# A one-core attention and MLP kernel: the second matrix product of the last eight chunks by Strassen's scheme, in two passes of its own

## The chip, the cores and the metric

The kernel runs on one core of a Trainium2 chip. The time is the device time of one execution in microseconds (us), with the median of several runs. Five engines work side by side and wait for each other through semaphores: PE (matmuls; its weight loads are shown apart as PEld), DVE and ACT (element-wise work), POOL, and SP, which here only issues DMAs. Every engine carries out its instructions in order.

## The reference

```python
for b in range(nb):                       # linear attention with decay, 4 x 8 heads, 768 x 64
    intra = einsum('bhic,bhjc->bhij', qb, kb) * Dmask
    out[:, :, sl] = einsum('bhij,bhjd->bhid', intra, vb) + einsum('bhid,bhde->bhie', qb * lam_pow, kv_state)
    kv_state = lam_block * kv_state + einsum('bhsd,bhse->bhde', kb_dec, vb)
x = out as 3072 tokens x 512
h = x @ w_in                              # 512 x 2048
g = maximum(h, 0) ** 2
return g @ w_out                          # 2048 x 512
```

## The kernel before

The 3072 tokens are 24 chunks of 128 (`t`); four chunks that are worked on together have a number `m` (0 to 5). The 2048 hidden features are 16 blocks of 128 (`f`). For precision each fp32 operand of a matmul is held as a high part in the matmul format fp32r and a low part, and a product is three matmuls: high x high, high x low, low x high. The weights lie so in `wh` and `wl` in SBUF: slots 0 to 15 for w_in, the others for w_out (`w_out(f)`, L106).

For m = 0 and 1 (chunks 0 to 7) `hidden` (L389) makes h of one f with 12 matmuls and `project` (L417) adds g @ w_out of that f into four PSUM banks `acc` with another 12 of 512 columns. For chunks 8 to 15 (m = 2 and 3 together) and 16 to 23 (m = 4 and 5) the first product goes by Strassen's scheme: `quad` (L561) takes a pair of f and pairs of neighbouring chunks as a 2 x 2 block product and needs seven products (`product`, L547, six matmuls of 512 columns each) where eight would stand. The sums of w_in blocks come from DRAM (`ws`) through a ring of eight tiles (`ring`, `stream`, tag "raw" of the pool `wk`), a load per product, eight products ahead. A quad ends with h of the even chunks in two PSUM banks, pa and pb, which ACT turns into g (Relu, Square) and DVE into a high and a low part (`square`, `rest`), and with g of the odd chunks kept in SBUF (`gs`). p1 is a copy of the first product; DVE adds it to others (u2, u3, and into pb). Between the products stand the projections of the quad before; the odd chunks are projected afterwards, f by f (`again`, then `project`), and in that stretch of m = 3 the attention of the next eight chunks is done.

The order on each engine is the order in which the code calls the operations. A tile of a pool takes one of the places of its tag, and what first writes it waits until the place's tile before is done with; tag "A" of `wk` has two places. When an m is through, `project` copies the four banks into two tiles o of tag "A" (`stage`; ACT takes banks 0 and 2, DVE 1 and 3) and SP stores them. This last `project` of an m runs inside the next `quad`, between its second and third product. Its p1 has tag "a".

Of the kernel before, what the change touches and what calls it, by code (L numbers as in the profile page):

```python
# [7 lines left out]
F32 = mybir.dt.float32  # L8
# [7 lines left out]
P = 128  # L16
B, H, S, D = 4, 8, 768, 64
C = 128
# [17 lines left out]
def body(ctx: ExitStack, tc: tile.TileContext, qT, kT, kvq, lam, w, out):  # L36
# [526 lines left out]

    def quad(n, m, prev, then=None):
# [22 lines left out]
        add(gs[1], pd, u3)  # L587
        rest(m, f, pa, gh)
# [5 lines left out]
        gh = square(pb)  # L594
        add(gs[0], pd, u2)
        rest(m, f + 1, pb, gh)
        for x in gs[::-1]:
            V.scalar_tensor_tensor(out=x, in0=x, scalar=0.0, in1=x, op0=ALU.max, op1=ALU.mult)  # L598
        project(m, f)
        return m, f + 1  # L600

# [217 lines left out]
    for m in range(2, NM, 2):  # L819
        more = m + 2 < NM  # L820
        first_t, last_t = (m + 2) * G, (m + 4) * G - 1
        for n in range(NF // 2):
            then = (lambda: load_kv(first_t)) if more and n == NF // 2 - 1 else None
            prev = quad(n, m, prev, then)
        again(m + 1, 0)
        if more:
            load_kv(first_t + 1)
            prep_k(first_t)
            scores(first_t, ps_a, "att")
            prep_q(first_t)  # L830
            masked(first_t)
        for f in range(NF):
            t = first_t + f // 2
            i, odd_ = f // 4, f // 2 % 2
            project(*prev)
            prev = (m + 1, f)
            if more and f % 2 == 0:
                if not odd_:
                    pack = wk.tile([P, 2, DM], F32, name="pack", tag="raw")
                KEPT[t] = pack[:, odd_]  # L840
                if t < last_t:
                    attend(t, ps_h, "h", t + 1)
                else:
                    attend(t, ps_a, "att")
                if t + 2 <= last_t:
                    load_qk(t + 2)
                    load_kv(t + 2)
            if f + 1 < NF:
                again(m + 1, f + 1)
            if more:  # L850
                if f % 2 == 0:
                    ahead(f + 1, t, last_t)
                    behind(f + 1, t, last_t)
                if f % 4 == 1:
                    part(*even(i, t))
                if f % 4 == 2:
                    part(*near(i, t - 1))
# [3 lines left out]
        if more:  # L861
            open_ring()
# [54 lines left out]
```

## Time and profile before

| | |
|---|---|
| median of 3 runs | 606.29 us (606.08 to 606.29) |
| the profiled execution | 606.06 us |
| its span, first to last instruction | 604.4 us |
| granted PE clock | 1.00 |
| PE, PEld, DVE, ACT, POOL busy | 98%, 81%, 58%, 39%, 15% |

The page's first part gives each engine's busy time, the fourth the chain of work that ended last, the fifth groups of instructions (line, engine, operation, output<-inputs, shape, count, busy us, mean ns of one, idle time before them and what ended it). A row of a timeline has the start, the length, the instruction and its count. The stretch with chunks 16 to 23 (m = 4 and 5) begins at about 435 us. A matmul's length is its time in the pipeline; the next one starts before it has ended.

### The profile page before, as it was taken

Reading aid. Unit: us, or ns where it says so; the run is one execution under the profiler, and the core shown is the slowest. Engines: PE = TensorE matmul, PEld = TensorE weight load, DVE = VectorE, ACT = ScalarE, POOL = GpSimd, SP = SyncE. Lnnn points to the kernel's source line nnn. Section 1 sums busy time; section 2 is a strip of 40 time slices with the busy share of each in tenths; the row PEclk is TensorE's granted clock in tenths of the full one; section 3 lists DMA queues with packets and bytes.
Section 4 is the critical chain, followed back from the end, with each engine's and each line's share of the span. In section 5 each row is a group of like instructions: output and inputs, shape, how many; then the busy total and the mean of one; then the engine's idle time right before and its main releaser. Section 6 shows DMA issues by size and latency. Waiting matters only on the chain.

```text
span 604.4 us, 9423 instructions
## 1 busy us (share of the span) xinstructions
PE 595.0 (98%) x3694; PEld 491.0 (81%) x3694; DVE 351.0 (58%) x535; ACT 235.6 (39%) x383; POOL 88.2 (15%) x95
## 2 busy tenths in 40 slices
PE   8989999999999999999999999999999999999997
PEld 6877888888888888888888888888888888888885
DVE  6899999938575677644444445766554444445222
ACT  4667887724333345432222222323332222223222
POOL 5411222323221231000000002243100000000000
PEclk9999999999999999999999999999999999999999
DMA  8766667227678674544444404432284444421001
GB/s 297 296 209 210 191 228 233 88 89 266 230 248 286 226 239 156 175 125 123 126 125 125 143 9 167 140 121 90 71 279 124 123 123 124 126 77 70 1 1 69
DMA packets 50107, 92.88 MB, mean 154 GB/s; under 512 B 5008, under 2 KB 19344, under 8 KB 50064
## 3 DMA queue, kind: packets, MB, share of 16 engines
q1 hardware_dynamic: 50064, 92.29, 47.6%
q8 instruction: 29, 0.48, 0.3%
q14 instruction: 14, 0.11, 0.1%
HBM read 71.30 MB, written 20.97 MB: 153 GB/s over the span
## 4 chain that ended last, share of the span: by engine, by line
PE 92%; DVE 5%; POOL 1%; ACT 1%; issue 0%; POOLq 0%; DVEq 0%
PE h L555 18%; PE acc L425 14%; PE acc L430 14%; PE acc L426 14%; PE h L395 13%; PE att L555 7%; PE att L279 3%; PE h L318 2%; PE h L325 2%; DVE A L138 1%; PE h L310 1%; DVE wl L153 1%; DVE A L144 1%; PE att L318 1%; DVE A L131 1%; PE att L325 1%
## 5 line engine op out<-in xcount | busy, mean ns | idle before, releaser
L425 PE MATMUL acc<-wh,gh 128*128 128x512 f32 x384 | 151.0, 393 | 0.0
L426 PE MATMUL acc<-wl,gh 128*128 128x512 f32 x384 | 149.5, 389 | 0.0
L430 PE MATMUL acc<-wh,gl 128*128 128x512 f32 x384 | 149.3, 390 | 0.0
L402 ACT ACTIVATE h<-h 128x512 f32<-128x512 f32 x64 | 37.3, 582 | 182.8 <-PE h L555 76.3
L555 PE MATMUL h<-wh,ring 128*128 128x512 f32 x320 | 85.5, 389 | 0.0
L425 PEld LDWEIGHTS acc<-wh,gh 128*128 128x128 f32 x384 | 72.0, 188 | 16.4 <-issue 0.5
L430 PEld LDWEIGHTS acc<-wh,gl 128*128 128x128 f32 x384 | 72.1, 188 | 15.7 <-DVE gl L410 0.5
L426 PEld LDWEIGHTS acc<-wl,gh 128*128 128x128 f32 x384 | 72.1, 188 | 14.6
L410 DVE TENSOR_TENSOR gl<-h,gh 128x512 fp32r<-128x512 f32 x64 | 44.1, 690 | 66.9 <-ACT h L405 66.8
L555 PEld LDWEIGHTS h<-wh,ring 128*128 128x128 f32 x320 | 60.1, 188 | 12.5
L208 DVE TENSOR_TENSOR kv_sb<-h,a 128x512 f32<-128x512 f32 x32 | 22.1, 691 | 64.7 <-PE h L555 63.1
L555 PE MATMUL h<-wl,ring 128*128 128x512 f32 x160 | 49.2, 389 | 0.0
L410 DVE TENSOR_TENSOR gl<-gs,gh 128x512 fp32r<-128x512 f32 x32 | 23.5, 736 | 42.5 <-ACT gh L605 42.0
L292 POOL TENSOR_TENSOR kv_sb<-kv_sb,mask 128x512 f32<-128x512 f32 x18 | 22.2, 1234 | 122.1 <-DVE gs L598 108.8
L404 ACT ACTIVATE gh<-h 128x512 fp32r<-128x512 f32 x64 | 38.4, 600 | 2.0
L405 ACT ACTIVATE h<-h 128x512 f32<-128x512 f32 x64 | 38.0, 594 | 0.0
L605 ACT CAST gh<-gs 128x512 fp32r<-128x512 f32 x32 | 19.9, 622 | 45.0 <-PE acc L426 45.0
L286 POOL TENSOR_TENSOR qk_sb<-qk_sb,qpow 128x512 f32<-128x512 f32 x18 | 27.0, 1500 | 68.9 <-PE att L279 67.9
L395 PE MATMUL h<-xh,wh 128*128 128x512 f32 x128 | 36.0, 403 | 0.0
L555 PEld LDWEIGHTS h<-wl,ring 128*128 128x128 f32 x160 | 30.0, 188 | 6.2
L395 PE MATMUL h<-xh,wl 128*128 128x512 f32 x128 | 34.5, 391 | 0.4 <-DVE wl L153 0.4
L395 PE MATMUL h<-xl,wh 128*128 128x512 f32 x128 | 34.3, 390 | 0.0
(141 smaller groups left out, 775.0 us busy)
## 6 DMA issues: line engine op xcount, KB each, us to landing
ring<-ws SPq DMA_DIRECT2D x112, 256.0 KB, 2.8
raw<-in_w SPq DMA_DIRECT2D x32, 512.0 KB, 4.6
kv_sb<-in_kvq SPq DMA_DIRECT2D x22, 512.0 KB, 5.2
ws<-parts SPq DMA_DIRECT2D x32, 256.0 KB, 2.7
out_x<-o SPq DMA_DIRECT2D x24, 256.0 KB, 2.2
qk_sb<-in_kT SPq DMA_DIRECT2D x22, 256.0 KB, 3.5
qk_sb<-in_qT SPq DMA_DIRECT2D x22, 256.0 KB, 4.2
ws<-wh SPq DMA_DIRECT2D x8, 256.0 KB, 5.2
```

What stands on the lines that cost most here:

```text
L208: lambda o, x, y, op=op: V.tensor_tensor(out=o, in0=x, in1=y, op=op)
L286: nc.gpsimd.tensor_tensor(out=feat[t][:, 1], in0=feat[t][:, 1], in1=qpow, op=ALU.mult)
L292: nc.gpsimd.tensor_tensor(out=x, in0=x, in1=y.broadcast_to([P, NPR, 2, D]), op=ALU.mult)
L395: nc.tensor.matmul(h, wt[:, f, kt * P : (kt + 1) * P], x[:, kt], start=k == 0, stop=k == 11)
L402: nc.scalar.activation(h, h, AF.Relu)
L404: nc.scalar.activation(gh, h, AF.Square)
L405: nc.scalar.activation(h, h, AF.Square)
L410: V.tensor_tensor(out=gl, in0=r, in1=gh.bitcast(F32), op=ALU.subtract)
L425: nc.tensor.matmul(accs[m][i], gh[:, cs], wh[:, j], start=f == 0, stop=False)
L426: nc.tensor.matmul(accs[m][i], gh[:, cs], wl[:, j], start=False, stop=False)
L430: nc.tensor.matmul(accs[m][i], gl[:, cs], wh[:, j], start=False, stop=end)
L555: nc.tensor.matmul(bank, x[:, part_, kt], t[:, q + kt], start=start and z == 0, stop=stop and z == 5, skip_group_check=True,)
```

## The change

Three things change.

1. **Chunks 8 to 15**: every `quad` gets a `fold(n)`: DVE rebuilds the two w_out blocks of the pair of f and makes four sums of their column halves, ACT (`fold_hi`) and DVE (`fold_lo`) split them into high and low parts, and SP stores both to DRAM (`wt`).
2. **Chunks 16 to 23, first product**: `quad_all` takes the place of `quad`. It projects nothing but the last of m = 3; g of the even chunks goes into SBUF places that are free by then (`E`; two of them through a tile "kept" and a DMA). Its p1 has tag "A".
3. **Chunks 16 to 23, second product**: `gather_all`, after all eight pairs, replaces the `project` calls of m = 4 and 5. Two passes (even chunks, odd chunks), in each eight pairs of f, seven products per pair, each of them six matmuls of 256 columns into one of seven banks. `operands` makes four sums of blocks of g, `operands_hi` and `operands_lo` their high and low parts, two pairs ahead and in three places of the old w_in slots; the w_out sums come back from `wt` through the two "raw" places, two pairs ahead. At the end of a pass seven adds form the output from the banks.

```diff
+    wt = dram.tile([NF // 2, P, 4, 2, 2 * P], F32, name="wt")
+    FOLD = {}
+
+    def fold(n):
+        rec = wk.tile([P, 2, 2, 2 * P], F32, name="rec", tag="A")
+        for i in range(2):
+            j = w_out(2 * n + i)
+            add(rec[:, i].rearrange("p b c -> p (b c)"), f32(wh[:, j]), f32(wl[:, j]))
+        x = wk.tile([P, 4, 2 * P], F32, name="sums", tag="A")
+        (b11, b12), (b21, b22) = ([rec[:, i, j] for j in range(2)] for i in range(2))
+        T1, T2, T3, T4 = (x[:, i] for i in range(4))
+        sub(T1, b12, b11)
+        sub(T2, b22, T1)
+        sub(T3, b22, b12)
+        sub(T4, b21, T2)
+        FOLD[n] = x
+
+    def fold_hi(n):
+        nc.scalar.copy(wh[:, NF - 2 : NF].rearrange("p a d -> p (a d)"), FOLD[n].rearrange("p a b -> p (a b)"))
+
+    def fold_lo(n):
+        hi, lo = (t[:, NF - 2 : NF].rearrange("p a d -> p (a d)") for t in (wh, wl))
+        sub(lo, FOLD.pop(n).rearrange("p a b -> p (a b)"), f32(hi))
+        for i, x in enumerate((hi, lo)):
+            nc.sync.dma_start(out=wt[n, :, :, i], in_=f32(x).rearrange("p (a b) -> p a b", a=4))
+
     def quad(n, m, prev, then=None):
...
         add(gs[1], pd, u3)
+        fold(n)
...
+        fold_hi(n)
...
+        fold_lo(n)
         project(m, f)
...
+    def square_to(f, h):
+        x = wk.tile([P, N], F32, name="kept", tag="A") if f in (2, 3) else E[f]
+        nc.scalar.activation(h, h, AF.Relu)
+        nc.scalar.activation(x, h, AF.Square)
+        if f in (2, 3):
+            nc.sync.dma_start(out=E[f], in_=x)
+
+    def places_for(f):
+        if f == 0:
+            E.extend(wk.tile([P, N], F32, name="kept", tag="a") for _ in range(2))
+            E.extend(f32(t[:, NF - 1]) for t in (wh, wl))
+            E.extend(mask.rearrange("p j a c -> p j (a c)")[:, j] for j in range(2))
+            E.extend(x.rearrange("p a c -> p (a c)") for x in (qpow, kv))
+        if f in (8, 10):
+            x = io.tile([P, 2 * DM], F32, name="qk_sb")
+            E.extend(x[:, j * DM : (j + 1) * DM] for j in range(2))
+        if f >= 12:
+            for _ in range(2):
+                E.append(wk.tile([P, N], F32, name="kept", tag="gh" if f == 12 else "gl"))
+
+    def quad_all(n, prev):
+        f = 2 * n
+        last = n == NF // 2 - 1
+        if n % 2 == 0:
+            G_of[n // 2] = wk.tile([P, 4, N], F32, name="gs", tag=("xh", "xl")[n // 2 % 2])
+        gs = [G_of[n // 2][:, f % 4 + j] for j in range(2)]
+        pa, pb = (ps_h.tile([P, N], F32, name="h") for _ in range(2))
+        pd = ps_a.tile([P, N], F32, name="att")
+        p1 = wk.tile([P, N], F32, name="p1", tag="A")
+        u23 = io.tile([P, 2, N], F32, name="kv_sb")
+        u2, u3 = u23[:, 0], u23[:, 1]
+        product(n, 0, pa, True, False)
+        nc.scalar.copy(p1, pa)
+        product(n, 1, pb, True, False)
+        add(u2, pb, p1)
+        if prev is not None:
+            project(*prev)
+        places_for(f)
+        product(n, 2, pd, True, False)
+        if last:
+            open_folds(0)
+        product(n, 3, pb, False, False)
+        add(u3, pb, p1)
+        product(n, 4, pa, False, True)
+        square_to(f, pa)
+        add(gs[1], pd, u3)
+        if last:
+            operands_hi(0)
+            operands_lo(0)
+        product(n, 5, pb, False, True)
+        product(n, 6, pd, False, True)
+        add(pb, pb, p1)
+        square_to(f + 1, pb)
+        add(gs[0], pd, u2)
+        for x in gs[::-1]:
+            V.scalar_tensor_tensor(out=x, in0=x, scalar=0.0, in1=x, op0=ALU.max, op1=ALU.mult)
+        if n == NF // 2 - 2:
+            operands(0)
+        if last:
+            open_folds(1)
+            for step in (operands, operands_hi, operands_lo):
+                step(1)
+
+    NQ = NF // 2
+
+    def open_folds(q):
+        TR[q] = wk.tile([P, 4, DM], F32R, name="folds", tag="raw")
+        for j in range(4):
+            fold_in(q, j)
+
+    def fold_in(q, j):
+        if q < 2 * NQ:
+            nc.sync.dma_start(
+                out=f32(TR[q % 2][:, j]), in_=wt[q % NQ, :, (1, 0, 2, 3)[j]].rearrange("p a b -> p (a b)")
+            )
+
+    def operands(q):
+        par, n = q // NQ, q % NQ
+        f = 2 * n
+        x0, x1 = (G_of[n // 2][:, f % 4 + j] if par else E[f + j] for j in range(2))
+        y0, y1 = (x.rearrange("p (r s c) -> p r s c", r=2, s=2) for x in (x0, x1))
+        (a11, a21), (a12, a22) = ([y[:, :, j] for j in range(2)] for y in (y0, y1))
+        s_ = wk.tile([P, 4, 2, C], F32, name="sums", tag="A")
+        S1, S2, S3, S4 = (s_[:, i] for i in range(4))
+        add(S1, a21, a22)
+        sub(S2, S1, a11)
+        sub(S3, a11, a21)
+        sub(S4, a12, S2)
+        OPS[q] = a11, s_.rearrange("p a r c -> p (a r c)"), x1
+
+    def region(q, t):
+        b = (q + 2) % 3 * 7 * 2 * C
+        return t[:, 0 : NF - 2].rearrange("p a d -> p (a d)")[:, b : b + 7 * 2 * C]
+
+    def cut(x, a11):
+        a = x[:, 0 : 2 * C]
+        return (a.rearrange("p (r c) -> p r c", r=2) if a11 else a), x[:, 2 * C : 10 * C], x[:, 10 * C : 14 * C]
+
+    def operands_hi(q):
+        for o_, x in zip(cut(region(q, wh), True), OPS[q]):
+            nc.scalar.copy(o_, x)
+
+    def operands_lo(q):
+        for o_, x, h in zip(cut(region(q, wl), True), OPS.pop(q), cut(region(q, wh), True)):
+            sub(o_, x, f32(h))
+
+    WHERE = [(0, C), (4 * C, C), (2 * C, C), (6 * C, C), (10 * C, 2 * C), (11 * C, 2 * C), (8 * C, C)]
+
+    def gather(q, i, bank):
+        n = q % NQ
+        f = 2 * n
+        if i in (0, 4, 6):
+            j, c = w_out(f + (i > 0)), 2 * P * (i == 6)
+            hi, lo = (t[:, j, c : c + 2 * P] for t in (wh, wl))
+        else:
+            j = i - 1 if i < 4 else 3
+            hi, lo = (TR[q % 2][:, j, h * 2 * P : (h + 1) * 2 * P] for h in range(2))
+        base, step = WHERE[i]
+        for r in range(2):
+            gh, gl = (region(q, t)[:, base + r * step : base + r * step + C] for t in (wh, wl))
+            for z, (x, y) in enumerate(((gh, hi), (gh, lo), (gl, hi))):
+                nc.tensor.matmul(
+                    bank[:, r * 2 * P : (r + 1) * 2 * P], x, y, start=n == 0 and r == 0 and z == 0,
+                    stop=n == NQ - 1 and z == 2, skip_group_check=True,
+                )
+        if i not in (0, 4, 6):
+            fold_in(q + 2, j)
+
+    def put_out(par, two, half, x):
+        o_ = out[NT * C - 2 * G * C :].rearrange("(r s w p) d -> p r s w d", r=2, s=2, w=2)
+        nc.sync.dma_start(out=o_[:, :, two, par, half * 2 * P : (half + 1) * 2 * P], in_=x.rearrange("p (r d) -> p r d", r=2))
+
+    def gather_all():
+        for par in range(2):
+            banks = []
+            for i in range(7):
+                if par:
+                    pool, name = ((ps_h, "h"), (ps_acc, "acc"), (ps_a, "att"))[(i > 0) + (i > 4)]
+                else:
+                    pool, name = ((ps_acc, "acc"), (ps_a, "att"), (ps_h, "h"))[(i > 3) + (i > 5)]
+                banks.append(None)
+                banks[i] = pool, name
+            for n in range(NQ):
+                q = par * NQ + n
+                end = n == NQ - 1
+                for i in range(7):
+                    if n == 0:
+                        pool, name = banks[i]
+                        banks[i] = pool.tile([P, DM], F32, name=name)
+                    gather(q, i, banks[i])
+                    if i == 0 and q + 2 < 2 * NQ:
+                        for step in (operands, operands_hi, operands_lo):
+                            step(q + 2)
+                    if not end:
+                        continue
+                    if i == 0:
+                        p1c = wk.tile([P, 2, DM], F32, name="p1", tag="A")
+                        p1, c = p1c[:, 0], p1c[:, 1]
+                        nc.scalar.copy(p1, banks[0])
+                        u23 = io.tile([P, 2, DM], F32, name="kv_sb")
+                        u2, u3 = u23[:, 0], u23[:, 1]
+                        o12 = [io.tile([P, 2, DM], F32, name="qk_sb") for _ in range(2)]
+                    if i == 1:
+                        add(u2, banks[1], p1)
+                    if i == 2:
+                        add(c, banks[2], u2)
+                    if i == 3:
+                        add(u3, banks[3], u2)
+                        add(o12[0][:, 0], banks[2], u3)
+                        put_out(par, 1, 1, o12[0][:, 0])
+                    if i == 4:
+                        add(o12[0][:, 1], banks[4], p1)
+                        put_out(par, 0, 0, o12[0][:, 1])
+                    if i == 5:
+                        add(o12[1][:, 0], banks[5], u3)
+                        put_out(par, 1, 0, o12[1][:, 0])
+                    if i == 6:
+                        add(o12[1][:, 1], banks[6], c)
+                        put_out(par, 0, 1, o12[1][:, 1])
...
+    open_ring()
+    for n in range(NF // 2):
+        quad_all(n, prev)
+        prev = None
+    gather_all()
```

Three places show how instructions move. In names, o is an output tile, `h` a PSUM bank of the first product, `acc` one of the second; the number behind a name tells buffers of one name apart; DMAHW, PE, DVE and Activation behind "waits" are the semaphores of DMAs and engines.

The first is the first pair of f for chunks 16 to 23, on DVE. Before, from u2 (kv_sb) over the two output copies to the pb add:

```order
L208 TENSOR_TENSOR kv_sb_3914<-h_3911,a_3913 128x512 [waits DMAHW1_49,DMAHW3_49,PE_49,DMAHW5_49,Activation_49,Pool_49]
L436 COPY o_3934<-acc_3295 128x512 [waits PE_49]
L436 COPY o_3945<-acc_3297 128x512 [waits DVE_49,PE_49]
L208 TENSOR_TENSOR kv_sb_3914<-h_3911,a_3913 128x512 [waits PE_49]
L208 TENSOR_TENSOR gs_3909<-att_3912,kv_sb_3914 128x512 [waits DVE_49]
L410 TENSOR_TENSOR gl_3980<-h_3910,gh_3976 128x512 [waits Activation_49]
L208 TENSOR_TENSOR h_3911<-h_3911,a_3913 128x512 [waits PE_49]
```

Now:

```order
L208 TENSOR_TENSOR kv_sb_4011<-h_4008,p1_4010 128x512 [waits DMAHW1_49,DMAHW3_49,PE_49,DMAHW5_49,Activation_49,Pool_49]
L436 COPY o_4031<-acc_3392 128x512 [waits DVE_49,PE_49]
L436 COPY o_4042<-acc_3394 128x512 [waits DMAHW0_49,DVE_49,DMAHW7_49,PE_49,Activation_49]
L208 TENSOR_TENSOR kv_sb_4011<-h_4008,p1_4010 128x512 [waits PE_49]
L208 TENSOR_TENSOR gs_4006<-att_4009,kv_sb_4011 128x512 [waits DVE_49]
L208 TENSOR_TENSOR h_4008<-h_4008,p1_4010 128x512 [waits PE_49]
```

The copy into the second output tile (o_4042) now waits for two DMAs: p1 holds one of the tag's two places, so this tile is laid on that of o_4031, whose stores are those DMAs. ACT's copy into o_4042 has the same wait; there it stands ahead of the Relu of pa:

```order
L665 COPY p1_4010<-h_4007 128x512 [waits DMAHW0_49,DMAHW7_49,PE_49,Activation_49]
L438 COPY o_4031<-acc_3391 128x512 [waits DMAHW1_49,DMAHW2_49,DVE_49,PE_49]
L438 COPY o_4042<-acc_3393 128x512 [waits DMAHW0_49,DVE_49,DMAHW7_49,PE_49,Activation_49]
L635 ACTIVATE h_4007<-h_4007 128x512 [waits PE_49]
L636 ACTIVATE kept_4050<-h_4007 128x512 [waits Activation_49]
```

The second place is the first pair for chunks 8 to 15, on DVE, from the gs add on. Before:

```order
L208 TENSOR_TENSOR gs_2400<-att_2403,kv_sb_2405 128x512 [waits DVE_49]
L410 TENSOR_TENSOR gl_2471<-h_2401,gh_2467 128x512 [waits Activation_49]
L208 TENSOR_TENSOR h_2402<-h_2402,a_2404 128x512 [waits PE_49]
L208 TENSOR_TENSOR gs_2400<-att_2403,kv_sb_2405 128x512 [waits PE_49]
L410 TENSOR_TENSOR gl_2493<-h_2402,gh_2489 128x512 [waits Activation_49]
```

Now:

```order
L208 TENSOR_TENSOR gs_2401<-att_2404,kv_sb_2406 128x512 [waits DVE_49]
L208 TENSOR_TENSOR rec_2472<-wh_90,wl_91 128x512 [waits DMAHW4_49,DMAHW3_49,Activation_49]
L208 TENSOR_TENSOR rec_2472<-wh_90,wl_91 128x512
L208 TENSOR_TENSOR sums_2475<-rec_2472 128x256 [waits DMAHW5_49,DMAHW6_49,DVE_49,Activation_49]
L208 TENSOR_TENSOR sums_2475<-rec_2472,sums_2475 128x256 [waits DVE_49]
L208 TENSOR_TENSOR sums_2475<-rec_2472 128x256
L208 TENSOR_TENSOR sums_2475<-rec_2472,sums_2475 128x256 [waits DVE_49]
L410 TENSOR_TENSOR gl_2480<-h_2402,gh_2468 128x512 [waits Activation_49]
L208 TENSOR_TENSOR h_2403<-h_2403,a_2405 128x512 [waits PE_49]
```

Six instructions of `fold` have come between the gs add and the low part gl of the same f.

The third is the switch to the second product: the end of the last pair and the first pair of the first pass, on PE. The adds and copies that the first rows wait for are shown behind it, on DVE, from the add u3 of the last pair to the four sums of the next operand set.

```order
L555 MATMUL att_4510<-wl_91,ring_3997 128x512 x2
L754 MATMUL acc_4596<-wh_90 128x256 [waits Activation_49]
L754 MATMUL acc_4596<-wl_91,wh_90 128x256
L754 MATMUL acc_4596<-wh_90,wl_91 128x256 [waits DVE_49]
L754 MATMUL acc_4596<-wh_90 128x256
L754 MATMUL acc_4596<-wl_91,wh_90 128x256
L754 MATMUL acc_4596<-wh_90,wl_91 128x256
L754 MATMUL acc_4614<-folds_4535,wh_90 128x256 [waits DMAHW3_49,Activation_49]
L754 MATMUL acc_4614<-folds_4535,wh_90 128x256
L754 MATMUL acc_4614<-folds_4535,wl_91 128x256 [waits DVE_49]
```

```order
L208 TENSOR_TENSOR kv_sb_4512<-h_4509,p1_4511 128x512 [waits PE_49]
L208 TENSOR_TENSOR gs_4435<-att_4510,kv_sb_4512 128x512 [waits DVE_49]
L208 TENSOR_TENSOR wl_91<-kept_4050,wh_90 128x256 [waits Activation_49]
L208 TENSOR_TENSOR wl_91<-sums_4503,wh_90 128x1024 [waits Activation_49]
L208 TENSOR_TENSOR wl_91<-kept_4051,wh_90 128x512 [waits Activation_49]
L208 TENSOR_TENSOR h_4509<-h_4509,p1_4511 128x512 [waits PE_49]
L208 TENSOR_TENSOR gs_4435<-att_4510,kv_sb_4512 128x512 [waits PE_49]
L688 SCALAR_TENSOR_TENSOR gs_4435<-gs_4435 128x512 [waits DVE_49] x2
L208 TENSOR_TENSOR sums_4585<-wh_90,wl_91 128x256 [waits DMAHW5_49]
L208 TENSOR_TENSOR sums_4585<-sums_4585,wh_90 128x256 [waits DVE_49]
L208 TENSOR_TENSOR sums_4585<-wh_90 128x256
L208 TENSOR_TENSOR sums_4585<-wl_91,sums_4585 128x256 [waits DVE_49]
```

What stood at the end before, the projections `acc<-wh,gh 128x512`, is gone; each product has six matmuls of 256 columns (an "x2" or a row each), and the low parts of the next operand set (wl) stand on DVE behind all adds of the last pair.

More of the change, by code (lines that the diff above doesn't have):

```diff
@@ L598, in quad @@
             V.scalar_tensor_tensor(out=x, in0=x, scalar=0.0, in1=x, op0=ALU.max, op1=ALU.mult)
+        fold_lo(n)
         project(m, f)
         return m, f + 1
+    E, OPS, TR = [], {}, [None, None]
+    def square_to(f, h):
[16 more added lines that the diff above has]
+                E.append(wk.tile([P, N], F32, name="kept", tag="gh" if f == 12 else "gl"))
@@ L817, in body @@
             part_lo(*x)
[L819 to L857, printed above, removed]
-                if f % 4 == 3:
-                    part(*far(i, t - 1))
-                    part(*last(i, t - 1))
-        if more:
-            open_ring()
@@ L863, in body @@
-    project(*prev)
+    m, first_t, last_t = 2, 4 * G, 6 * G - 1
+    for n in range(NF // 2):
+        prev = quad(n, m, prev, (lambda: load_kv(first_t)) if n == NF // 2 - 1 else None)
+    again(m + 1, 0)
+    load_kv(first_t + 1)
+    prep_k(first_t)
+    scores(first_t, ps_a, "att")
+    prep_q(first_t)
+    masked(first_t)
+    for f in range(NF):
+        t = first_t + f // 2
+        i, odd_ = f // 4, f // 2 % 2
+        project(*prev)
+        prev = (m + 1, f)
+        if f % 2 == 0:
+            if not odd_:
+                pack = wk.tile([P, 2, DM], F32, name="pack", tag="raw")
+            KEPT[t] = pack[:, odd_]
+            if t < last_t:
+                attend(t, ps_h, "h", t + 1)
+            else:
+                attend(t, ps_a, "att")
+            if t + 2 <= last_t:
+                load_qk(t + 2)
+                load_kv(t + 2)
+        if f + 1 < NF:
+            again(m + 1, f + 1)
+        if f % 2 == 0:
+            ahead(f + 1, t, last_t)
+            behind(f + 1, t, last_t)
+        if f % 4 == 1:
+            part(*even(i, t))
+        if f % 4 == 2:
+            part(*near(i, t - 1))
+        if f % 4 == 3:
+            part(*far(i, t - 1))
+            part(*last(i, t - 1))
@@ L866, in _limit @@
+    open_ring()
+    for n in range(NF // 2):
+        quad_all(n, prev)
+        prev = None
+    gather_all()
 def _limit():
```

## The prediction

> **What bounds the kernel now.** I read the page's busy shares first, then its chain, then the stages of the second half.
>
> ```profile
> span 604.4 us, 9423 instructions
> PE 595.0 (98%) x3694; PEld 491.0 (81%) x3694; DVE 351.0 (58%) x535; ACT 235.6 (39%) x383; POOL 88.2 (15%) x95
> ...
> PE 92%; DVE 5%; POOL 1%; ACT 1%; issue 0%; POOLq 0%; DVEq 0%
> ...
> 480.00:520.00 40.00, 40.00 (x178) 33.10 (x178) 14.87 (x22) 10.12 (x18) 0.00 (x0) 1.00 0.46 126
> 560.00:604.00 44.00, 40.33 (x178) 33.05 (x177) 11.08 (x16) 9.29 (x15) 0.00 (x0) 1.00 0.06 24
> ```
>
> The matmul engine carries 92% of the chain. The two last rows are stages (length, busy of PE, weight loads, DVE, ACT, POOL, granted clock): from 480 to 520 PE never rests, at full clock, and DVE and ACT are busy for 15 and 10 of 40 us. So a matmul saved is time saved, unless PE is then made to wait. The change does both.
>
> The profiled execution took 606.06 us, 1.7 more than its span and 0.2 under the median of the three runs (606.29). I add to 606.06.
>
> **Fewer matmuls.** These are products of the w_in phase, six 512-column matmuls each, and the three w_out lines.
>
> ```profile
> 441.05 1.07 PE L555 MATMUL h<-wh,ring 128*128 128x512 f32 x4
> 441.96 0.61 PE L555 MATMUL h<-wl,ring 128*128 128x512 f32 x2
> 442.41 1.07 PE L555 MATMUL h<-wh,ring 128*128 128x512 f32 x4
> 443.32 0.61 PE L555 MATMUL h<-wl,ring 128*128 128x512 f32 x2
> 443.77 1.07 PE L555 MATMUL h<-wh,ring 128*128 128x512 f32 x4
> ...
> L425 PE MATMUL acc<-wh,gh 128*128 128x512 f32 x384 | 151.0, 393 | 0.0
> 7.75 0.94 PE L247 MATMUL h<-pz 128*128 128x128 f32 x7
> L247 PE MATMUL h<-pz x16: 275/275/421, 5.8 to 8.4; 128*128 128x128 f32 x16
> 9.72 1.15 PE L260 MATMUL att<-pz,odd 8*128 8x128 f32 x8
> ```
>
> A product starts every 1.36 us, so a 512-column matmul takes 0.2267 (the 393 ns are its length in the pipeline). The last eight chunks are a third of the 384 on each of three lines: 384 matmuls, 87.0 us. In their place stand 2 passes x 8 pairs of f x 7 products x 6 = 672 matmuls of 256 columns. No row has that shape. Half of 0.2267 is 0.113; but each matmul also loads 128 columns of weights, twice as often per column now. The two small shapes with a 128-column load run at (0.94 - 0.275)/6 = 0.111 and (1.15 - 0.27)/7 = 0.126. I take **0.120**, the middle of 0.113 and 0.126: 80.6 us, **-6.4**. The ends give -11.1 and -2.3.
>
> The Trainium skill, "TensorE: Matmul & The Clock Gate", section "Back-to-back issue gap", has 262 cycles at 2.4 GHz for 256 columns, an estimate of 0.109 us and 73.4 for the 672. Its 518 cycles (0.216) for 512 columns are below the 0.2267 here, so the trace does not bear it out.
>
> **fold in the first pair of chunks 8 to 15.** The w_out sums are made on DVE, ahead of the low part gl of the same f.
>
> ```profile
> 252.15 0.69 DVE L208 TENSOR_TENSOR gs<-att,kv_sb 128x512 f32<-128x512 f32 x1
> 254.52 0.69 DVE L410 TENSOR_TENSOR gl<-h,gh 128x512 fp32r<-128x512 f32 x1 [1.68 <-ACT h L405]
> 255.76 0.39 PE L430 MATMUL acc<-wh,gl 128*128 128x512 f32 x1
> ...
> 160.38 0.42 DVE L208 TENSOR_TENSOR sums<-rec 128x256 f32<-128x256 f32 x1
> 161.52 0.41 DVE L208 TENSOR_TENSOR sums<-rec,sums 128x256 f32<-128x256 f32 x1
> 163.66 1.23 DVE L208 TENSOR_TENSOR parts<-sums,parts 128x1024 fp32r<-128x1024 f32 x1 [0.26 <-ACT parts L479]
> L523 DVE TENSOR_TENSOR wl<-pack,wh 128x512 fp32r<-128x512 f32 x4 | 2.7, 683 | 0.0
> ```
>
> Two adds of 512 (1.3) and four of 256 (160.38 to 161.93: 1.55) follow 252.84, then gl: done at 256.4 with the hand-off, where PE wants it at 255.76: **+0.6**. In the other seven pairs a projection of 2.7 us stands between, and the 4.2 us of DVE fit into 15 us. The stores of the sums (1 MB per pair) delay ring loads that run eight products ahead; I cost them at nothing, and a late ring would show as PE waiting for a DMA.
>
> **The stores of chunks 12 to 15, the largest term.** In the first pair of the last eight chunks p1 now lies in the pool's tag A, whose two places also take the two output tiles of the last projection. One place is p1's until this pair is nearly done, so the second output tile (rows o_4042) gets the place of the first (o_4031) and its copies wait for that tile's two stores to land. Behind the waiting copy on DVE stands the u3 add, for which product 5 waits; on ACT the Relu of product 4.
>
> ```profile
> 441.59 2.73 SPq L440 DMA_DIRECT2D out_x<-o  x4
> 442.07 0.38 SPq L440 DMA_DIRECT2D out_x<-o  x1
> DMA to landing us min/median/max: 6.1/6.1/6.1
> 442.61 0.69 DVE L208 TENSOR_TENSOR kv_sb<-h,a 128x512 f32<-128x512 f32 x1 [2.03 <-PE h L555]
> out_x<-o SPq DMA_DIRECT2D x24, 256.0 KB, 2.2
> ```
>
> The stores leave late because six ring loads stand ahead on SP, and these still do. The second leaves at 442.07 and lands 6.1 later, 448.2. Copy 0.69, add 0.69 and hand-offs: product 5 starts at 449.7. Today it starts at 443.77 (the row above): **+5.9**. If the store landed as most do, in 2.2, it would be 2.0; those are the ends. After it the chain through pb (add, Relu, Square, about 2.1 us) fits the 2.72 of two products, so the following pairs run free.
>
> **The start of the second phase.** Counted from the end of the last w_in product. Operand set q (a pair of f in one pass) needs four sums on DVE (1.55), the high cast of 1024 on ACT, the low part of 1024 on DVE (1.23) and one of 512.
>
> ```profile
> L479 ACT CAST parts<-sums 128x1024 fp32r<-128x1024 f32 x8 | 8.4, 1044 | 2.3 <-DVE sums L208 2.3
> L519 ACT CAST wh<-pack 128x256 fp32r<-128x256 f32 x4 | 1.6, 400 | 0.0
> L577 ACT COPY a<-h 128x512 f32<-128x512 f32 x16 | 9.4, 588 | 40.1 <-PE h L555 40.1
> L402 ACT ACTIVATE h<-h 128x512 f32<-128x512 f32 x64 | 37.3, 582 | 182.8 <-PE h L555 76.3 <-PE h L395 60.1 <-DVE h L208 46.3
> ```
>
> The sums of set 0 stand before the last pair's u2 add, which product 3 needs: +0.3. Set 0's casts start on ACT behind the Relu and Square of product 4, at -1.3, and its 1024 low part is done at 1.3, where product 1's third matmul wants it at 0.96: +0.45. Only then come on DVE the pb add, the gs add, two squares (to 4.5), the sums of set 1 (6.0), after ACT's cast (7.05) its low part (8.3). Set 1's first matmuls are due at 5.5: PE waits 0.7 for the low 256 and 1.2 for the low 1024. In all **+2.7**.
>
> **The turn between the passes.** From there a set costs DVE and ACT in turn 1.55 + 1.04 + 1.23 + 0.65, about 4.45, against 42 x 0.120 = 5.04 on PE, so the lateness is worked off by 0.6 a set. Set 9, asked for in the last set of the first pass, is done at 8.9 + 8 x 4.45 = 44.5, and only behind it come the copy of bank 0 (43.7 on ACT) and the adds that free the other banks. The second pass starts at 42.7: product 1 waits 0.4 for bank 0, product 2 0.8, product 3 1.3 (c, u3 and an output add read bank 2): **+2.5**. Stores and the last add are as today: the last DVE copy starts 0.4 behind the last matmul, and one follows now too; nothing there.
>
> **The sum:** -6.4 + 0.6 + 5.9 + 2.7 + 2.5 = +5.3, **611.4**. At 0.113 a matmul the waits grow as the matmuls shrink (2.7 and 4.4 for the last two): 608.9. At 0.126 they shrink: 613.3.
>
> **Rivals.**
> *The clock drops in the wait.* 5.9 us without a matmul is longer than any gap of this trace.
>
> ```profile
> 2.39 3.62 PE L63 MATMUL att<-kv 128*128 128x512 f32 x5
> 5.81 0.63 PE L247 MATMUL h<-pz 128*128 128x128 f32 x2
> 18.92 1.16 PE L279 MATMUL acc<-lent 64*128 64x128 f32 x16 [1.07 <-DMA lent<-in_qT]
> ```
>
> At the start PE works slowly until about 6.8 us (two L247 take 0.2 apiece, the later ones 0.111); a gap of 1.07 did not bring that back. Were it to come back for the same 5.4 us at half speed, 2.7 more: 614.1. The Trainium skill's same page, Part 1, says one idle window of about 3.4 us halves the clock; by that rule this is what happens. No row has such a gap, so it gets 0.25.
>
> *The wait is hidden* (the other side). If SP gets the stores out right behind their copies and they land in about 2, they are gone before product 5: 605.5. It decides at a wait of 1.8 us, below which the whole is within 0.2%. For it: 2.2 is the usual landing. Against it: the six loads and the 441.59. 0.15.
>
> *A cheap matmul*, 0.113 or less: 608.9, since DVE and ACT then bound the phase. 0.13. A dear one (0.126) belongs to my case's upper end.
>
> **How the numbers follow.** Forecast 0.42 (its own range 609.5 to 613.3), clock 0.25, cheap matmul 0.13, hidden wait 0.15, 0.05 outside. 0.2% (1.2 us) is about what a measurement of this kernel tells from no change. Hidden wait together with a cheap matmul would be faster: 0.07; hidden alone, the same: 0.09; slower 0.84. The range, 606.5 to 615.0, leaves out the hidden wait and what lies above the clock case.
>
> **What would show it.** A PE gap of about 6 us before product 5 of the first pair of the last eight chunks, with DVE L436 waiting for out_x; granted clock below 1 behind it or not; L754 matmuls 0.120 apart where nothing waits; gaps on L754 in the first two sets and at the second pass's start; 0.6 at the first L430 of chunks 8 to 15. No gap before product 5 makes it wrong.

## The result, and the profile after

| | time, us (median, lowest to highest) | profiled run: time, span, clock |
|---|---|---|
| before | 606.29 (606.08 to 606.77, 4 runs) | 606.06, 604.4, 1.000 |
| changed | 614.95 (614.54 to 616.47, 4 runs) | 615.24, 613.5, 0.994 |

The changed kernel takes 1.0146 times as long, 95% interval 1.0128 to 1.0165. The direction was forecast; the sum of 611.4 was 3.6 low. The time lies above the 609.5 to 613.3 that the sum allowed itself, 0.05 under the top of the whole range (615.0), and beside the rival in which the clock drops (614.1).

The first lines of the page of the changed kernel; of part 2 only the granted clock (40 slices of the span, in tenths):

```profile
span 613.5 us, 10384 instructions
PE 593.9 (97%) x3982; PEld 501.5 (82%) x3982; DVE 423.8 (69%) x681; ACT 253.8 (41%) x405; POOL 87.3 (14%) x95
...
PEclk9999999999999999999999999999979999999999
```

PE's 288 further matmuls are the 672 short ones less the 384 long ones. Its busy time still fell by 1.1 us (from 595.0), so the loss is waiting, and one slice of the clock line, a 7, says that some of the busy time ran slow. What PE waits for, from 230 us to the end of the changed kernel (line waited for, us in total, times, longest):

```profile
PE h L555 <- DVE kv_sb L208: 5.8, 1, 5.8
PE acc L754 <- DVE wl L208: 1.0, 2, 0.8
PE acc L754 <- DVE kv_sb L208: 0.9, 2, 0.5
PE acc L754 <- DMA folds<-wt: 0.5, 1, 0.5
PE acc L754 <- ACT p L791: 0.3, 1, 0.3
PE acc L430 <- DVE gl L410: 0.2, 1, 0.2
```

In the kernel before this view has no row in that stretch. The first line is one wait in the first pair of the last eight chunks. PE's timeline there (start, us), then what DVE, ACT and SP do at that place, then the same place in stretches (length, busy of PE, weight loads, DVE, ACT and POOL, granted clock, share of DMA and GB/s):

```profile
444.53 0.61 PE L555 MATMUL h<-wl,ring 128*128 128x512 f32 x2
450.94 2.08 PE L555 MATMUL h<-wh,ring 128*128 128x512 f32 x4 [5.79 <-DVE kv_sb L208]
...
456.10 1.09 PE L555 MATMUL h<-wh,ring 128*128 128x512 f32 x4
```

```profile
443.01 7.96 SPq L440 DMA_DIRECT2D out_x<-o  x4
...
449.59 0.69 DVE L436 COPY o<-acc 128x512 f32<-128x512 f32 x1 [8.81 <-DMA out_x<-o]
450.20 0.68 DVE L208 TENSOR_TENSOR kv_sb<-h,p 128x512 f32<-128x512 f32 x1
...
449.55 0.59 ACT L438 COPY o<-acc 128x512 f32<-128x512 f32 x1 [9.64 <-DMA out_x<-o]
```

```profile
444.70:450.90 6.20, 0.45 (x2) 0.03 (x1) 1.29 (x2) 1.32 (x3) 0.00 (x0) 0.86 0.50 174
450.90:455.80 4.90, 4.86 (x12) 3.80 (x12) 1.39 (x2) 1.48 (x3) 0.00 (x0) 0.50 0.94 299
455.80:459.00 3.20, 3.20 (x15) 2.64 (x14) 1.89 (x3) 0.64 (x2) 0.00 (x0) 0.98 0.48 125
```

Product 4's last matmul starts at 444.76 and product 5 at 450.94, 6.18 later instead of 0.23: 5.95 lost. DVE's copy into the second output tile waits for the stores of the first, as the prediction named it, and the u3 add (kv_sb), for which PE waits, stands behind that copy. Then the clock is 0.50, and the next two products (12 matmuls) take 450.94 to 456.10, 5.16 instead of 12 x 0.2267 = 2.72: another **2.44**. PE counts as busy all that while, which is why busy shares don't show it. From the clock column, the half speed lasted 2 x (0.14 x 6.20 + 0.50 x 4.90 + 0.02 x 3.20) = 6.8 us, of which the first 1.7 lay in the wait.

### The profile page after: what moved, and what is told of

Read it like the earlier page. It is cut to its first block, busy times and chain, and to the rows that moved or that the text cites. A ratio compares the mean times of both kernels' runs of the same rounds, so it can differ in the third digit from the quotient of the medians.

```text
span 613.5 us, 10384 instructions
## 1 busy us (share of the span) xinstructions
PE 593.9 (97%) x3982; PEld 501.5 (82%) x3982; DVE 423.8 (69%) x681; ACT 253.8 (41%) x405; POOL 87.3 (14%) x95
## 4 chain that ended last, share of the span: by engine, by line
PE 50%; DVE 4%; DMA 2%; ACT 1%; issue 0%; SPq 0%; DVEq 0%; ACTq 0%
PE h L555 16%; PE att L555 7%; PE acc L425 5%; PE acc L754 5%; PE acc L430 5%; PE acc L426 5%; PE att L754 3%; PE att L279 1%; DVE wl L208 1%; PE h L754 1%; PE h L318 1%; DMA folds<-wt 1%; DMA out_x<-o 1%; ACT wh L733 1%; DVE sums L208 1%; PE h L325 1%
## 5 line engine op out<-in xcount | busy, mean ns | idle before, releaser
L425 PE MATMUL acc<-wh,gh 128*128 128x512 f32 x256 | 101.2, 395 | 0.0
L430 PE MATMUL acc<-wh,gl 128*128 128x512 f32 x256 | 100.0, 391 | 0.2 <-DVE gl L410 0.2
L426 PE MATMUL acc<-wl,gh 128*128 128x512 f32 x256 | 99.7, 389 | 0.0
L402 ACT ACTIVATE h<-h 128x512 f32<-128x512 f32 x48 | 28.0, 584 | 119.5 <-PE h L395 53.2
L425 PEld LDWEIGHTS acc<-wh,gh 128*128 128x128 f32 x256 | 48.0, 188 | 11.3 <-issue 0.7
L430 PEld LDWEIGHTS acc<-wh,gl 128*128 128x128 f32 x256 | 48.0, 188 | 11.2 <-DVE gl L410 1.0
L208 DVE TENSOR_TENSOR wl<-sums,wh 128x1024 fp32r<-128x1024 f32 x24 | 29.4, 1223 | 13.2 <-ACT wh L733 13.2
L754 PE MATMUL acc<-folds,wh 128*128 128x256 f32 x192 | 36.0, 286 | 1.7 <-DVE kv_sb L208 0.9
L555 PE MATMUL att<-wh,ring 128*128 128x512 f32 x128 | 35.0, 396 | 0.0
L754 PEld LDWEIGHTS acc<-folds,wh 128*128 128x128 f32 x192 | 29.8, 191 | 2.9 <-DVE kv_sb L208 1.3
```

What stands on the lines that cost most here:

```text
L208: lambda o, x, y, op=op: V.tensor_tensor(out=o, in0=x, in1=y, op=op)
L402: nc.scalar.activation(h, h, AF.Relu)
L425: nc.tensor.matmul(accs[m][i], gh[:, cs], wh[:, j], start=f == 0, stop=False)
L426: nc.tensor.matmul(accs[m][i], gh[:, cs], wl[:, j], start=False, stop=False)
L430: nc.tensor.matmul(accs[m][i], gl[:, cs], wh[:, j], start=False, stop=end)
L555: nc.tensor.matmul(bank, x[:, part_, kt], t[:, q + kt], start=start and z == 0, stop=stop and z == 5, skip_group_check=True,)
```

## The experiments

Every kernel ran beside the kernel before on its chip; that kernel's median was 606.6 to 606.8 in these sessions. Times are medians.

**p1 out of the output tiles' places.**

```diff
-        p1 = wk.tile([P, N], F32, name="p1", tag="A")
+        if n:
+            p1 = wk.tile([P, N], F32, name="p1", tag="A")
+        else:
+            p1 = io.tile([P, 2, N], F32, name="qk_sb")[:, 0]
```

> In the first pair of the last eight chunks p1 takes half of a qk_sb buffer, which is free there, and no place of tag A; nothing else differs from the changed kernel (614.95). Theory: the collision of p1 with the two output tiles makes the 6.18 us from product 4 to product 5, and the wait makes the half clock behind it. Then both go: products 4 and 5 start 1.36 apart, the granted clock stays at 1.0 after 440, and the time falls by 5.95 + 2.44 to 606.6 (606.0 to 607.2). Rival A: the half clock has another cause than the wait (the kind of work there): the gap goes, the clock still drops, about 609.0. Rival B: another wait for the same stores takes its place on the copies: 610 to 613.

607.47 (606.25 to 609.75, 10 runs; 606.8 before; ratio 1.0016, interval 1.0003 to 1.0029), profiled at 606.25. The row of 440 to 460 of this kernel, columns as above:

```profile
440.00:460.00 20.00, 20.00 (x90) 16.53 (x89) 9.94 (x16) 6.49 (x11) 0.00 (x0) 1.00 0.92 311
```

PE is busy for the whole of it, at full clock. One buffer's place made both the wait and the half clock: rivals A and B fall. The profiled time is 9.0 less than the changed kernel's, of which 8.4 was expected; that the wait of set 10 is absent in this profile (below) covers the rest. The median fell by 7.5 only, to 0.9 above the 606.6 expected, with three of ten runs over 608.5.

**Matmuls into the wait: 22, 6 and 14 of them.** The result of the fillers is not used.

```diff
+        if n == 0:
+            spare = ps_a.tile([P, N], F32, name="att")
+            for _ in range(22):
+                nc.tensor.matmul(spare, wh[:, 0, 0:P], wh[:, 0], start=True, stop=True, skip_group_check=True)
         product(n, 5, pb, False, True)
```

> 22 matmuls of 512 columns into a spare bank, between products 4 and 5 of the first pair of the last eight chunks; the result is not used. The wait of product 5 is left as it is; 22 x 0.2267 = 4.99 of its 6.18 us now have matmuls in them, and 1.2 us are left without. Theory (the half clock comes from the time without matmuls): the granted clock stays at 1.0 there, the matmuls behind the wait stand 0.2267 apart, and the time falls by 2.44 to 612.5 (612.1 to 612.9). Rival (the slow matmuls come from what stands behind the wait, such as the transfers or the late chain on DVE and ACT): no change, 614.5 to 615.3.

> The same with 6 matmuls: 1.36 of the 6.18 us are filled, and 4.6 from the last filler's end stay empty. If every gap beyond some length under 4.6 us halves the clock, all runs show a granted clock of about 0.993 and 614.5 to 615.3. If 4.6 is too short, all show 1.0 and about 612.5. If it depends on where the gap falls in a window that runs freely, the runs differ: some at 612.5 with clock 1.0, some at 615 with 0.993; the Trainium skill, TensorE: Matmul & The Clock Gate, Part 1, says this last, with a window of about 3.4 us, by which about a third of the runs would drop, an estimate from that figure.

> 14 fillers: 3.17 of the 6.1 to 7.0 us between products 4 and 5 are filled, and 2.9 to 3.9 from the last filler on stay empty, between the 1.98 that kept the clock and the 5.56 that lost it. The lengths of the half and full clock in every trace so far, taken from their records, are whole multiples of 3.413 us, so that a whole such stretch has to be empty: with under 3.4 empty no run drops (clock 1.0, 612.5 to 615, as the 22 fillers), and with up to 3.9 one run in seven at most. If half of such a stretch empty is enough, most runs drop (0.993 to 0.996, 615 to 617).

With 22: 614.78 (614.29 to 616.01; granted clock of the four runs 0.997 to 1.000). With 6: 616.97 (616.17 to 617.24; 0.993 to 0.995). With 14: 614.21 (613.63 to 615.99; 0.996 or 0.997). PE's timelines: the fillers (L685), product 5, and the product that starts 12 matmuls after it. With 22, 14 and 6:

```profile
445.24 5.15 PE L685 MATMUL att<-wh 128*128 128x512 f32 x22
451.97 1.19 PE L555 MATMUL h<-wh,ring 128*128 128x512 f32 x4 [1.59 <-DVE kv_sb L208]
...
454.83 1.07 PE L555 MATMUL h<-wh,ring 128*128 128x512 f32 x4
```

```profile
444.76 3.33 PE L685 MATMUL att<-wh 128*128 128x512 f32 x14
451.10 2.07 PE L555 MATMUL h<-wh,ring 128*128 128x512 f32 x4 [3.01 <-DVE kv_sb L208]
...
455.38 1.08 PE L555 MATMUL h<-wh,ring 128*128 128x512 f32 x4
```

```profile
445.58 1.52 PE L685 MATMUL att<-wh 128*128 128x512 f32 x6
452.27 2.07 PE L555 MATMUL h<-wh,ring 128*128 128x512 f32 x4 [5.17 <-DVE kv_sb L208]
...
457.56 1.21 PE L555 MATMUL h<-wh,ring 128*128 128x512 f32 x4
```

The 12 matmuls take 2.86 behind 1.6 us of emptiness, 4.28 behind 3.0 and 5.29 behind 5.2, with the same work, transfers and late engines around them. So the lack of matmuls makes the half clock, as the rival of the prediction and the rule of the Trainium skill ("TensorE: Matmul & The Clock Gate", Part 1) had it. All four runs with 6 fillers lost the clock, where the rule with one whole idle window gave about a third of them, and all four with 14 are below the 0.998 to 1.000 of the kernel before, where it gave one in seven at most: the rule as the expectations took it is too strict (last section), though the 614.21 is under the 615 to 617 of the case that came. But the total of the 22 fillers missed its 612.5 and lies where the rival had it; the clock speaks against that rival, the time alone does not. The wait itself came out longer: in this profile product 5 starts 6.73 after the first filler, which is product 4's end, where the changed kernel has 450.94 - 444.99 = 5.95, and PE waits 1.7 for a transfer in set 10, where it was 0.5. What the clock gave, slower transfers took. The 616.97 with 6 fillers, above all that was expected, has the same cause in its profile: its stores landed in 7.2 instead of 5.9. Whether the fillers make the transfers slower or the runs differ was asked by running the changed kernel again.

**The changed kernel again.**

> The changed kernel once more, beside the kernel before on this chip: the fillers of 22 and 6 matmuls gave 614.8 and 617.0 there, where 612.5 and 615 were expected from 614.95, and in both the first output tile's stores landed 7.3 after their issue instead of 5.9, and set 10 waited 1.85 and 1.3 instead of 0.98. Theory (transfer times differ by up to 2 us from run to run, whatever the kernel; the half clock costs 2.4): 614.5 to 617.5, landing between 5.5 and 7.5, clock 0.993 to 0.995. Rival (the fillers themselves make the stores late and hide what the clock gives): 614.5 to 615.3 and landing 5.9, as before.

> The changed kernel, with the stores of the last projection of chunks 12 to 15 issued on ACT right behind their copies and not on SP behind six ring loads. Both stores of the first tile then leave near 440.0 and 440.9 instead of 443.0 and 443.5. If SP's order is what made them late (2.2 to landing, as most output stores): they land by 443.5, no gap of over 0.5 is left and no half clock: about 607. If the transfers themselves are slow beside the eight ring loads (5.9 to 7.3 to landing, as measured): they land at 446.5 to 448, the gap is 3.5 to 5, and the time falls by 1.5 to 2.6 without the clock, by up to 5 with it: 610 to 613.5.

The second of these was meant to issue stores elsewhere, but its condition named a projection that the kernel does not have, so it is the changed kernel once more. The first gave 615.57 (615.36 to 616.81; ratio 1.0147, interval 1.0132 to 1.0162), the second 616.25 (614.28 to 618.14; 1.0157, 1.0132 to 1.0183). The first profile has the stores landing in 6.1. In the second, without any filler, they landed in 7.4, the wait was 6.6 and the half clock lasted 2 x (0.30 x 7.10 + 0.50 x 6.00) = 10.3 us:

```profile
445.50:452.60 7.10, 0.47 (x4) 0.05 (x2) 1.32 (x3) 1.36 (x3) 0.00 (x0) 0.70 0.43 140
452.60:458.60 6.00, 6.00 (x14) 4.74 (x15) 1.85 (x3) 1.49 (x3) 0.00 (x0) 0.50 0.82 262
```

So the stores' landing varies from run to run without fillers too, as widely as with them: the expectation that transfers differ holds, and that the fillers add nothing is likely but not shown.

**The stores on ACT's queue.** `project` issues the output stores of chunks 12 to 15 with nc.scalar behind the copies, where SP had six ring loads ahead of them.

```diff
-                nc.sync.dma_start(out=out[t * C : (t + 1) * C, :], in_=o)
+                queue = nc.scalar if m == 3 else nc.sync
+                queue.dma_start(out=out[t * C : (t + 1) * C, :], in_=o)
```

> The stores of the last projection of chunks 12 to 15 issued on ACT behind their copies. In the run before, the condition named a projection that does not exist here (5; it is 3), so that kernel was the changed kernel once more: 616.25. Now it takes hold. If SP's order is what made the stores late: landed by 443.5, no gap over 0.5, no half clock, 606.5 to 608. If they are slow beside the eight ring loads, wherever they are issued: landed at 446.5 to 448, a gap of 3.5 to 5: 610 to 613.5.

609.96 (609.73 to 611.88; ratio 1.0059, interval 1.0039 to 1.008). Its timeline (PE's rows and ACT's queue; SP's ring loads run beside), and its view of these stores' transfers in the window:

```profile
439.82 1.24 ACTq L441 DMA_DIRECT2D out_x<-o  x2
...
444.41 0.61 PE L556 MATMUL h<-wl,ring 128*128 128x512 f32 x2
447.16 1.20 PE L556 MATMUL h<-wh,ring 128*128 128x512 f32 x4 [2.13 <-DVE kv_sb L208]
```

```profile
DMA to landing us min/median/max: 3.5/4.9/5.0
```

The stores leave 3.2 earlier and land about 5 after their issue: neither expectation alone. SP's order made three microseconds of the wait, and the slow landing beside the ring loads the rest; the 2.2 of a usual store is not to be had here. A wait of 2.1 in place of 5.8 is left, and in this profile the clock holds through it, so 3.7 us less of waiting bought 5.6 (615.57 to 609.96, beside 606.8 and 606.6). Of the other four runs one, 610.45, has a clock of 0.996, as the runs with 14 fillers have, so it may have lost the clock here; no profile of it tells.

**The first pass's stores behind set 10's loads.** From here on, p1 lies in qk_sb. The four stores of pass 1 are issued on SP after the fold loads of the next pair of f instead of ahead of them (a list `late`, put out behind product 6 of set 8).

> p1 in qk_sb as before, and the four stores of the first pass's output are issued on SP behind the loads of the w_out sums for set 10 instead of ahead of them. Theory: the wait of set 10 (0.98 in the changed kernel, 0 in the profiled run without the collision, 1.3 and 1.85 in two others) is made by these stores and is what spreads that kernel's runs from 606.3 to 609.8; then no gap over 0.35 stands in set 10 and the runs lie within 606.0 to 606.9. Rival (the spread comes from elsewhere, such as the loads' own landing times): the runs spread as before, median 607.5.

606.61 (605.79 to 607.50, 10 runs; ratio 0.9999, interval 0.9990 to 1.0008), without a gap in set 10, the runs wider apart than the 606.0 to 606.9 expected. The loads of the w_out sums that stand among and behind these stores, in the changed kernel (570 to 576), in the kernel with p1 moved and SP's order kept (561.4 to 567.4, the same place), and in the first repeat of the changed kernel (570.5 to 576.5), from the view of their transfers:

```profile
DMA to landing us min/median/max: 4.5/6.3/6.5
```

```profile
DMA to landing us min/median/max: 4.2/5.9/6.3
```

```profile
DMA to landing us min/median/max: 4.3/6.8/7.1
```

PE waits for them in the first (0.5) and the third (0.8), not in the second, though the stores stand ahead of its loads as well. So the order alone doesn't make the wait; it seems to put the loads at the edge, where the time they take to land decides. With the stores behind, the slowest of ten runs fell from 609.75 to 607.50, which fits; the runs of the kernel before spread as widely (606.04 to 608.24), so the 0.9 between the two medians is not all shown to be this wait.

**Another order at four places.**

```diff
-        fold(n)
         rest(m, f, pa, gh)
+        fold(n)
...
             operands_hi(0)
             operands_lo(0)
+            operands_hi(1)
+            operands_lo(1)
...
-                        for step in (operands, operands_hi, operands_lo):
+                        for step in (operands,) if end else (operands, operands_hi, operands_lo):
                             step(q + 2)
```

Beside these, the sums of set 1 are made at the end of the pair before the last, in a kv_sb buffer, fold_lo(7) stands behind the masks of the next chunk, and at the turn operands_hi(9) stands behind the copy of bank 0, operands_lo(9) behind the pass's last add.

> p1 in qk_sb, and four places put in another order: the w_out sums behind the low part of the same f (and the last pair's low part behind the masks); the sums, casts and low parts of set 1 ahead of the last pair's last adds; at the end of the first pass set 9's cast behind the copy of bank 0 and its low part behind the pass's seven adds. The first pass's stores stay where they were. Theory: the terms of the sum are order on DVE and ACT alone, so their gaps close: -0.5 before the first low part of chunks 8 to 15, -0.4 at the attention of chunks 12 to 15, -1.5 to -2.1 of 2.16 at the start of the second phase, -1.2 to -1.8 of 1.87 at the turn: 602.5 to 604.3, seen from 607.5. Rival (DVE and ACT are full there, and what closes here opens in a later set): 605.5 or more, with gaps in sets 2 to 4 or 9.

> All of these together: p1 in qk_sb, the stores of the first pass behind set 10's loads, and the new order at the four places. Theory: the terms add up: 601.8 to 603.5, faster than the kernel before by 0.5% to 0.8%. Rival (with the gaps closed the loads of the sums become the limit in the second pass): 604 or more, with PE waiting for the loaded sums in sets 9 to 12.

606.53 (606.08 to 607.14; ratio 0.9996, interval 0.9987 to 1.0004), and with the stores behind 606.38 (605.52 to 607.52; 0.9992, 0.9984 to 1.0001): no faster than the kernel before, and both theories missed. The turn closed: the stretch from 550 to 580 of the kernel with p1 moved, and of this one:

```profile
550.00:580.00 30.00, 28.84 (x233) 27.90 (x232) 24.50 (x48) 11.40 (x19) 0.00 (x0) 1.00 0.72 231
```

```profile
550.00:580.00 30.00, 30.00 (x253) 30.00 (x252) 25.36 (x50) 11.37 (x18) 0.00 (x0) 1.00 0.77 242
```

But PE's timeline of the new order (without the stores' part) has three waits that were not there:

```profile
262.03 1.19 PE L555 MATMUL h<-wh,ring 128*128 128x512 f32 x4 [1.45 <-DVE gl L410]
...
512.33 1.20 PE L555 MATMUL h<-wh,ring 128*128 128x512 f32 x4 [1.43 <-DVE kv_sb L208]
...
523.01 0.50 PE L762 MATMUL att<-folds,wh 128*128 128x256 f32 x2 [0.97 <-DVE gs L208]
```

Each is an instruction that I had put ahead of one that PE wants sooner: the sums ahead of the pb add of the same pair, the sums of set 1 ahead of the last pair's u2 add, its low part ahead of the gs add that frees a bank. Gaps were not closed but moved, as the first rival said, though to other places than it named and not because the engines are full there, as the next run shows. The loads of the sums, the second rival's limit, made no wait in these two profiles.

**The second try.** fold, fold_hi and fold_lo of pair n - 1 in pair n (of the last pair, during the attention of chunks 12 to 15); the sums of set 1, again in a kv_sb buffer, behind the last pair's first gs add, its cast behind set 0's, its low part behind the second gs add; turn and stores as in the run of all.

```diff
-        fold(n)
+        if n:
+            fold(n - 1)
...
+            operands(1)
             operands_hi(0)
             operands_lo(0)
+            operands_hi(1)
...
         add(gs[0], pd, u2)
+        if last:
+            operands_lo(1)
```

> The orders of the last two runs closed the gaps at the turn, but opened three others: 1.6 at the second pair of chunks 8 to 15 (the low part of f + 1 stands behind the sums), 1.6 at product 3 of the last pair (the sums of set 1 stand ahead of its u2 add), 1.1 in set 0 (the gs add stands behind the low part of set 1). Here p1 is in qk_sb and the first pass's stores and the turn are as in that last run; the w_out sums of pair n are made in pair n + 1, those of the last pair during the attention of chunks 12 to 15; the sums of set 1 stand behind the last pair's first gs add, its cast behind set 0's, its low part behind the second gs add. Theory: DVE and ACT have room for all of it, only not at the places chosen; then no gap over 0.5 is left from 230 to the end but about 0.1 and 0.3 at product 3 of the last pair and in set 0, and the time is 600.5 to 602.5, faster than before by 0.7% to 1.0%. Rival (the engines are full there): 605 or more, with new gaps on DVE's L208 or ACT's casts.

**602.07** (601.90 to 603.88; ratio **0.9933**, interval 0.9919 to 0.9947): faster than the kernel before, and inside the 600.5 to 602.5 expected. From 230 us to the end the view of waits is empty for PE (it leaves out small delays, such as one of 0.4 at the attention, below). Its page:

```profile
span 600.2 us, 10373 instructions
```

## Why the prediction was right or wrong

Terms as forecast, and as the profiled run of the changed kernel has them (starts of matmuls against the even spacing):

| term | forecast | measured |
|---|---|---|
| fewer matmuls | -6.4 | -6.4 |
| fold, first pair of chunks 8 to 15 | +0.6 | +0.5 |
| wait for the output tile's stores | +5.9 | +5.95 |
| half clock behind it | 0 (a rival, 0.25) | +2.4 |
| start of the second phase | +2.7 | +2.4 |
| turn between the passes | +2.5 | +2.0 |
| set 10 waits for its loads | not seen | +1.0 |
| attention of chunks 12 to 15 | not seen | +0.4 |
| tail | 0 | +0.5 |
| sum | +5.3 | +8.8 |

The profiled times differ by 9.2; of the 0.4 that is left, some 0.2 was lost before 205 us, where nothing is changed. The sum was about 3.5 low: 2.4 for the clock and 1.9 for three things not seen, less 0.9 for start, turn and fold, which were forecast a little dear.

**Fewer matmuls: right.** Twelve matmuls of bank h in the changed kernel, the first and the last:

```profile
564.78 0.28 PE L754 MATMUL h<-wh 128*128 128x256 f32 x1
...
566.10 0.28 PE L754 MATMUL h<-wh,wl 128*128 128x256 f32 x1
```

1.32 for eleven steps: 0.120 each, as taken between 0.113 and 0.126. The cheap and the dear matmul both fall, and so does the 0.109 estimated from the Trainium skill ("TensorE: Matmul & The Clock Gate", "Back-to-back issue gap"): the measurement decides.

**The stores: right** in place, cause and size; the run with p1 moved shows it. "The wait is hidden" falls.

**The clock: the step that failed.** The forecast gave the half clock nothing and its rival 0.25, because "No row has such a gap". That no row contradicts a rule is no reason to take a quarter for it: the trace showed slow matmuls at the start, the rule gave a length, and 5.9 us is longer than it. With the 2.4 in the sum the forecast would have been 613.8. The runs showed 6.8 us at half speed and 2.4 us lost in its place, and no loss once the wait was gone (p1 moved). The rival's own price, 2.7 from 5.4 us at half speed, was near, but partly by luck: the 5.4 was the length of the slow start, while here it was 6.8, of which 5.1 fell on work. That its 614.1 lies beside the result is luck as well, since the terms forecast too dear and those not seen partly cancel.

**Start and turn: right in place, a little dear.** The turn's three waits came as forecast at products 1, 2 and 3 of the second pass:

```profile
566.66 0.50 PE L754 MATMUL acc<-folds,wh 128*128 128x256 f32 x2 [0.28 <-ACT p L791]
...
568.12 0.50 PE L754 MATMUL acc<-folds,wh 128*128 128x256 f32 x2 [0.48 <-DVE kv_sb L208]
...
569.52 0.50 PE L754 MATMUL acc<-folds,wh 128*128 128x256 f32 x2 [0.42 <-DVE kv_sb L208]
```

**Three things not seen.** The queue behind a waiting instruction was followed for DVE and ACT, but not for SP at the turn: there the stores of pass 1, which wait for late adds, have set 10's loads behind them, which is likely, and not shown, to be a part of that wait's cause (above). In the attention of chunks 12 to 15 only the first pair was searched for fold; fold_lo of the last pair stands ahead of the masks. L318 wants both masked tiles; before, then after:

```profile
366.88 1.09 PE L318 MATMUL h<-a,kv_sb 128*64 128x128 f32 x16
367.80 1.04 PE L325 MATMUL h<-qk_sb,kv 128*64 128x128 f32 x16
```

```profile
363.94 1.22 DVE L208 TENSOR_TENSOR wl<-sums,wh 128x1024 fp32r<-128x1024 f32 x1
...
366.79 1.27 DVE L298 TENSOR_TENSOR a<-att,mask 128x512 f32<-128x512 f32 x2
```

The second mask ends at 368.06, where L318 has started at 367.67. In the run with fold_lo(7) behind the masks L318's 16 matmuls run through again; in the second try, in which pair 6's fold_lo stands at the old place, they don't, so it keeps that 0.4. And the tail: "one follows now too" held for the count of adds only. Four output adds of 0.6 stand in a row on DVE behind products that come 0.72 apart, and the first of them starts late:

```profile
608.63 0.28 PE L754 MATMUL att<-wh,wl 128*128 128x256 f32 x1
608.74 0.68 DVE L208 TENSOR_TENSOR qk_sb<-att,kv_sb 128x512 f32<-128x512 f32 x1
609.34 0.68 DVE L208 TENSOR_TENSOR qk_sb<-att,p 128x512 f32<-128x512 f32 x1
```

The last add starts 0.71 behind the last matmul, where a copy had started 0.4 behind it: 0.3 of the 0.5. This was not tried for itself.

What stays open is why the same transfer lands in 5.9 us in one run of the same kernel and in 7.4 in another, and so what share of the spread of 605.8 to 609.8 it makes.

## What to carry to other kernels

A buffer that moves to another pool tag waits for whatever lives in that tag: list the tag's tenants at that moment, and what must land before they leave. Price a wait of several microseconds on the matmul engine twice, once for itself and once for the slow matmuls behind it; cutting it to 2.1 here was worth more than its length, since the clock then mostly held. A saving of matmuls shows only when each instruction added on the other engines stands behind all that PE wants sooner, on SP as well; moving one by guess moves the gap.

## What the runs showed of the hardware

The clock's loss did not need the longest wait. In the profiled runs a wait of 3.0 us brought it (14 fillers), 2.1 (stores on ACT) and 1.6 (22 fillers) did not. The half speed came in steps: 3.4 us with 14 fillers, from the clock column of its row and of the one ahead of it, 6.8 in the changed kernel and 10.3 in its repeat with the longer wait.

```profile
447.70:451.10 3.40, 0.39 (x2) 0.00 (x0) 1.30 (x3) 1.35 (x3) 0.00 (x0) 0.95 0.09 34
451.10:454.30 3.20, 3.20 (x8) 2.54 (x9) 0.91 (x2) 0.32 (x1) 0.00 (x0) 0.52 0.91 303
```

2 x (0.05 x 3.40 + 0.48 x 3.20) = 3.4. It began 0.34 before product 5, at 450.76, and the fillers, at 0.2267 each from 444.76 on, were through at 447.93, so 2.8 us without a matmul were enough here; in the repeat 4.3 of the 10.3 lay before product 5, and it began 2.5 us after product 4's end. The rule of the Trainium skill ("TensorE: Matmul & The Clock Gate", Part 1) names one idle window of about 3.4 us; the steps agree with such a window, if one that is empty for some 2.5 to 2.8 of its 3.4 counts already. Where between 2.1 and 2.5 the limit lies, and whether the 2.1 was spared because it fell into two windows, isn't shown.

A 256-column matmul with a 128-column weight load costs 0.120, 0.53 of the 0.2267 of 512 columns: halving the columns costs 6%. And a 256 KB store beside the burst of 256 KB ring loads took 5.9 to 7.4 us to land from SP's queue and about 5 from ACT's, where the median of the kernel before is 2.2.
